# Local attention fused with a PReLU feed-forward network: half of each visit's block transfers go over GpSimd's queue

## The chip, the core and the metric

The program runs on one core of a Trainium2 chip. The core has four compute engines (PE, the matrix engine; DVE, the vector engine; ACT, the scalar engine; POOL, GpSimd) and SP (SyncE), which here only issues DMA transfers. Each engine works through its own instruction list in order; a transfer is issued by one of the engines, and then runs on the core's 16 DMA engines. The metric is the device time of one execution in microseconds.

## The reference

```
scores = (q_chunk @ k_chunk.T) / 8            # batch 8, 8 heads, seq 576, chunks of 64, head size 64
attn   = exp(scores - max); attn /= sum + 1e-9
x      = attn @ v_chunk                       # as a matrix: 4608 tokens x 512
h      = x @ w_in                             # 512 x 2048
g      = max(h, 0) + alpha * min(h, 0)
out    = g @ w_out                            # 2048 x 512
```

All data are float32. Attention is local: a chunk of 64 tokens looks only at itself.

## The kernel before

**Blocks.** The 4608 tokens are nine blocks of 512, and each block is four sub-blocks of 128 tokens (two chunks) for the attention. Sub-blocks 0 to 7 are done at the start in an order written out by hand (the list START). The other 28 are done in 28 *visits* that are woven into the feed-forward work.

**Stages.** Blocks 0 to 2 go through the plain feed-forward form, up to about 306 us: `first_layer` (L421) forms 128 hidden units for 512 tokens in a PSUM tile `ps_h`; ACT takes its negative part (L406), DVE completes the PReLU (L409), ACT rounds it to a high part gh (L435), DVE forms the low part gl (L438); `ffn_out` (L457) multiplies both with w_out into the result tiles ps_oa and ps_ob. At the end of a block (and of a part of one) `store` copies these four results out (L491 on ACT, for two of them sometimes L489 on DVE), and only then may PE write the next block's results there. Blocks 3 to 8 go in three pairs with a form of seven products in place of eight (`first_product` L719, `second_product` L847). Its weights are sums of quarters of w_in and w_out. They are made in the plain stage by `combine` (16 times: DVE L615, L622 to L625, ACT L631 and DVE L632, in the scratch tiles ta and tb and the buffers raw and more) and written to DRAM by POOL (`keep_a`, L593, four stores for each tile pair). The pair stages stream them back through a ring of four buffers (`stream`, L656, on POOL's queue); a load is issued when PE is done with the ring buffer that it goes into.

**A visit.** PE forms the values of the sub-block two visits earlier (`attn_values`, L388), which needs that sub-block's transposed probabilities `pT`, and then the scores of a new one (`attn_scores`, L272), in the one PSUM tile `ps_a`. DVE takes the row maximum (L284), ACT scales it (L285) and does eight exponentials (L287); ACT copies the values out of the same PSUM tile (L402 in the plain stage's first visits, with DVE's L403 for the low part; L399 later), and this copy (or L403) frees the tile for the next visit. DVE normalises (L289 to L291) and transposes 32x32 squares into a tile `t` (L331). `attn_blocks` then issues eight transfers (L338) of 32 partitions x 256 numbers (32 KB) each: chunk c, source half i, destination half j. They put the squares onto the right partitions in `pT`. Both t and pT have two buffers. 14 visits lie in the plain stage (136 to 286 us), 8 in the first pair stage (306 to 388 us), 6 in the second (464 to 538 us).

**Order.** PE's order is written in the code and pinned from the plain stage's step 20 on. The orders of DVE, ACT, POOL and SP are chosen when the kernel is built, by a scheduler that takes the instruction which is ready first in its own estimate of the times. So an edit to a transfer can move instructions of other engines. `combine` is tied behind the softmax of the latest visit; nothing else in the loop ties its rows to their place.

Of the kernel before, what the change touches and what calls it, by code (L numbers as in the profile page):

```python
# [59 lines left out]
def tile_local_attention_prelu_ffn(  # L60
# [12 lines left out]
    nc = tc.nc  # L73
# [253 lines left out]
    def attn_blocks(s):  # L327

        pr = probs.pop(s)
        tb = stage.tile([P, 2, H, HALF], F32, name="t3", bufs=2)  # L330
        nc.vector.transpose(tb.rearrange("p j h t -> p h j t"), pr)  # L331
        pT = load.tile([P, 2, H, HALF], F32, name="pT", bufs=2)
        for c in range(2):
            for i in range(2):
                for j in range(2):
                    src = slice(c * C + i * HALF, c * C + (i + 1) * HALF)
                    dst = slice(c * C + j * HALF, c * C + (j + 1) * HALF)
                    nc.sync.dma_start(  # L338
                        out=pT[dst, i].rearrange("p h t -> p (h t)"),
                        in_=tb[src, j].rearrange("p h t -> p (h t)"),  # L340
                    )
        pdiag[s] = pT
# [185 lines left out]
    def visit_results(old, xo, new, sc3):  # L528
        if old is not None:
            attn_x(old, xo)  # L530
        if new is not None:
            attn_blocks(new)
# [526 lines left out]
```

## Time and profile before

| | before |
|---|---|
| times of three runs, us | 774.68, 775.44, 777.26 (median 775.44) |
| the profiled execution, us | 775.11 |
| its span in the trace, us | 773.3 |
| outside the span, us | 1.8 |
| PE busy, us (share) | 761.3 (98%) |
| DVE busy, us | 648.2 (84%) |
| ACT busy, us | 448.9 (58%) |
| POOL busy, us | 184.9 (24%) |
| granted TensorE clock | 1.00 |

The span is the time from the first to the last instruction in the trace; the 1.8 us outside are the difference to the execution's own time. Busy time of an engine counts its compute instructions and, on POOL, the issue of its transfers; SP's issues are not counted. A wait is idle time of an engine just before an instruction, with what ended it.

### The profile page before, as it was taken

How to read it: one execution, taken by the hardware profiler on the slowest of the kernel's cores; microseconds unless marked ns; L12 is line 12 of the kernel's file. 1: busy time of each engine (PE TensorE's matmuls, PEld its weight loads, DVE VectorE, ACT ScalarE, POOL GpSimd, SP SyncE). 2: the span in 40 equal slices, each digit the busy share in tenths (PEclk: the TensorE clock that was granted, in tenths of full speed). 3: DMA queues.
4: the chain of work that ended last, by engine and by line, in shares of the span. 5: the costliest groups of instructions: out<-in, count | busy, mean ns of one | idle time of the engine just before them, and what ended most of it. 6: DMA issues, size and time to landing. Idle time of an engine off the chain costs nothing.

```text
span 773.3 us, 15417 instructions
## 1 busy us (share of the span) xinstructions
PE 761.3 (98%) x5558; PEld 640.4 (83%) x5558; DVE 648.2 (84%) x1140; ACT 448.9 (58%) x1221; POOL 184.9 (24%) x304
## 2 busy tenths in 40 slices
PE   7999999999999999999999999999999999999998
PEld 6788888887878888888888888888888888888886
DVE  6999989997989976877899898777898977679784
ACT  6975555566666665665756446655564544354642
POOL 1153322342425230111112111111122122112110
PEclk9999999999999999999999999999999999999999
DMA  9869595566969685878775678876656765565574
GB/s 355 328 198 386 180 322 206 182 228 192 267 209 272 219 287 168 304 272 279 264 239 204 232 243 286 267 235 212 207 201 218 253 236 191 200 208 192 197 253 148
DMA packets 69323, 184.53 MB, mean 239 GB/s; under 512 B 10992, under 2 KB 18176, under 8 KB 69120
## 3 DMA queue, kind: packets, MB, share of 16 engines
q0 software_dynamic: 34336, 119.56, 45.1%
q1 hardware_dynamic: 34480, 63.20, 24.0%
q8 instruction: 44, 0.72, 0.4%
q10 hardware_dynamic: 432, 0.79, 0.3%
q14 instruction: 31, 0.25, 0.1%
HBM read 135.27 MB, written 42.99 MB: 231 GB/s over the span
## 4 chain that ended last, share of the span: by engine, by line
PE 75%; DVE 6%; DMA 6%; ACT 5%; SPq 5%; issue 2%; POOL 0%; DVEq 0%; ACTq 0%
PE ps_o L719 19%; PE ps_o L847 19%; PE ps_h L719 10%; PE ps_h L847 10%; PE ps_h L421 6%; SPq L338 4%; PE ps_oa L457 4%; PE ps_ob L457 3%; DMA pT<-t 2%; PE ps_a L388 2%; DMA raw<-w_in 1%; ACT wi L313 1%; PE ps_a L272 1%; DMA raw<-w_out 1%; ACT wo L313 1%
## 5 line engine op out<-in xcount | busy, mean ns | idle before, releaser
L421 PE MATMUL ps_h<-xh,wi 128*128 128x512 f32 x384 | 101.6, 384 | 0.2 <-ACT xh L373 0.2
L421 PEld LDWEIGHTS ps_h<-xh,wi 128*128 128x128 f32 x384 | 70.8, 187 | 13.0 <-ACT xh L373 0.4
L719 PE MATMUL ps_o<-wi,raw 128*128 128x512 f32 x336 | 79.1, 382 | 0.0
L719 PEld LDWEIGHTS ps_o<-wi,raw 128*128 128x128 f32 x336 | 62.5, 187 | 11.2
L675 ACT CAST gh<-wo 128x512 fp32r<-128x512 f32 x66 | 41.0, 620 | 47.4 <-PE ps_o L847 31.8
L287 ACT ACTIVATE pr<-ps_a,mx 128x64 f32<-128x64 f32 x224 | 67.1, 326 | 0.9
L457 PE MATMUL ps_oa<-wo,gh 128*128 128x512 f32 x192 | 58.5, 385 | 0.3 <-ACT more L491 0.2
L457 PE MATMUL ps_ob<-wo,gh 128*128 128x512 f32 x192 | 57.8, 381 | 0.3 <-ACT g L491 0.3
L435 ACT CAST gh<-g 128x512 fp32r<-128x512 f32 x48 | 30.2, 630 | 35.3 <-DVE g L409 31.4
L421 PE MATMUL ps_h<-xl,wi 128*128 128x512 f32 x192 | 50.5, 381 | 0.0
L676 DVE TENSOR_TENSOR gl<-wo,gh 128x512 fp32r<-128x512 f32 x63 | 43.2, 685 | 7.6 <-ACT gh L675 7.1
L287 ACT ACTIVATION_READ_ACCUMULATOR pr<-ps_a,mx 128x1 f32 x224 | 48.9, 218 | 0.0
L656 POOL DMA_DIRECT2D raw<-wi_a x42 | 22.3, 531 | 98.0 <-PE ps_o L719 54.2
L656 POOL DMA_DIRECT2D raw<-wo_a x42 | 22.2, 529 | 90.8 <-PE ps_o L847 51.0
L406 ACT ACTIVATE wo<-gh 128x512 f32<-128x512 f32 x24 | 15.2, 632 | 48.4 <-DVE gh L749 48.4
L457 PEld LDWEIGHTS ps_ob<-wo,gh 128*128 128x128 f32 x192 | 35.8, 187 | 7.0 <-ACT g L491 0.7
L675 ACT CAST ta<-wo 128x512 fp32r<-128x512 f32 x42 | 26.1, 621 | 26.6 <-PE ps_o L847 15.4
L421 PEld LDWEIGHTS ps_h<-xl,wi 128*128 128x128 f32 x192 | 35.8, 187 | 6.6 <-DVE xl L375 0.2
L457 PEld LDWEIGHTS ps_oa<-wo,gh 128*128 128x128 f32 x192 | 35.4, 187 | 7.1 <-ACT more L491 0.6
L719 PE MATMUL ps_o<-wi,wi 128*128 128x512 f32 x168 | 40.4, 383 | 0.0
L719 PE MATMUL ps_o<-wi,wo 128*128 128x512 f32 x168 | 40.4, 383 | 0.0
L719 PE MATMUL ps_h<-wi,raw 128*128 128x512 f32 x168 | 40.4, 382 | 0.0
(298 smaller groups left out, 2037.7 us busy)
## 6 DMA issues: line engine op xcount, KB each, us to landing
raw<-wi_a POOLq DMA_DIRECT2D x42, 512.0 KB, 4.6
raw<-wo_a POOLq DMA_DIRECT2D x42, 512.0 KB, 3.5
wi<-wi_a POOLq DMA_DIRECT2D x21, 512.0 KB, 3.9
wo<-wi_a POOLq DMA_DIRECT2D x21, 512.0 KB, 4.0
wi<-wo_a POOLq DMA_DIRECT2D x21, 512.0 KB, 3.5
wo<-wo_a POOLq DMA_DIRECT2D x21, 512.0 KB, 3.8
k_sb<-kT SPq DMA_DIRECT2D x28, 256.0 KB, 4.4
q_sb<-qT SPq DMA_DIRECT2D x28, 256.0 KB, 3.8
```

Of the source, the lines that this page charges most:

```text
L287: last = nc.scalar.activation(pr[:, g], sc3[:, g // NP, g % NP], AF.Exp, bias=mx[:, g], scale=SCALE, accum_out=sm[:, g])
L313: last = nc.scalar.activation(pr[:, g], sc3[:, g % 2, g // 2], AF.Exp, bias=mx[:, g], scale=SCALE, accum_out=sm[:, g])
L338: nc.sync.dma_start(out=pT[dst, i].rearrange("p h t -> p (h t)"), in_=tb[src, j].rearrange("p h t -> p (h t)"),)
L388: pe(nc.tensor.matmul(att[0][par * C:(par + 1) * C, c, hp * C:(hp + 1) * C], lhsT=v_sb[rows, h * C:(h + 1) * C], rhs=p[rows, :, par * NP + ...
L421: pe(nc.tensor.matmul(woven(hps), lhsT=wi[f][:, l, k * P:(k + 1) * P], rhs=woven(xx[:, k]), start=(i == 0 and k == 0), stop=(i == 2 and k ...
L435: nc.scalar.copy(gh, g)
L457: pe(nc.tensor.matmul(woven(o), lhsT=a[:, ts], rhs=woven(wo[f][:, l]), start=(f == first and i == 0), stop=(f == last and i == 2),))
L656: streamed[0] = nc.gpsimd.dma_start(out=f32(t), in_=units[side][n])
L675: hi = nc.scalar.copy(t_hi, t)
L676: return hi, nc.vector.tensor_tensor(t_lo, t, f32(t_hi), op=ALU.subtract)
L719: pe(nc.tensor.matmul(woven(ps), lhsT=w[:, l, k * P:(k + 1) * P], rhs=woven(xx[:, xl]), start=first and at == 0, stop=at == n - 1, skip_gr ...
L847: pe(nc.tensor.matmul(woven(ps[m]), lhsT=w[:, l, m * P:(m + 1) * P], rhs=woven(xx), start=i in (1, 5, 2) and j == 0 and n == 0, stop=j == ...
```

## The change

In `attn_blocks`, a transfer whose source half i is 1 is issued by GpSimd, and one whose source half is 0 by SyncE as before. Four of a visit's eight transfers move, 112 of 224 in all. Their sizes, sources and destinations stay.

```diff
@@ -335,7 +335,7 @@
                 for j in range(2):
                     src = slice(c * C + i * HALF, c * C + (i + 1) * HALF)
                     dst = slice(c * C + j * HALF, c * C + (j + 1) * HALF)
-                    nc.sync.dma_start(
+                    (nc.gpsimd if i else nc.sync).dma_start(
                         out=pT[dst, i].rearrange("p h t -> p (h t)"),
                         in_=tb[src, j].rearrange("p h t -> p (h t)"),
                     )
```

The order of PE's 2392 rows is the same. The other engines' lists move as the scheduler chose.

On POOL the moved transfers stand in line with the stores of `keep_a`. This is the piece around the visits whose transposed tiles are t_1968 and t_2138 (about 160 to 175 us); wi_a_133 and so on are units of the combined weights in DRAM.

```order
 L593 DMA wi_a_133<-more 128x2x256 x2
 L593 DMA wi_a_135<-more 128x2x256 x2
+L338 DMA pT<-t_1968 32x256 x4
 L593 DMA wi_a_136<-raw 128x2x256
 L593 DMA wi_a_137<-raw 128x2x256
 L593 DMA wi_a_140<-raw 128x2x256 x2
+L338 DMA pT<-t_2138 32x256 x4
 L593 DMA wi_a_139<-raw 128x2x256
 L593 DMA wi_a_138<-raw 128x2x256
```

Two sets of four transfers now stand ahead of stores that followed each other before.

On ACT, a piece around the end of block 0's second part (about 170 to 177 us). ps_oa and ps_ob are the two result tiles; L631 are casts of `combine`.

```order
 L406 ACTIVATE g<-ps_h 128x512
 L631 CAST raw<-tb 128x512
-L631 CAST more<-ta 128x512
-L435 CAST gh<-g 128x512
-L406 ACTIVATE g<-ps_h 128x512
-L491 COPY more<-ps_oa 128x512 x2
 L435 CAST gh<-g 128x512
 L491 COPY ob<-ps_ob 128x512
 L491 COPY g<-ps_ob 128x512
+L631 CAST more<-ta 128x512
+L491 COPY more<-ps_oa 128x512 x2
 L285 ACTIVATE mx<-mx 128x8
```

The two copies that empty ps_oa stood ahead of an L435 and of the copies that empty ps_ob; they are now behind these and behind the cast of ta, which is the last product of a `combine`.

On DVE, about 265 to 272 us, the rows from the transposition of one visit to the row maximum (L284) of the next. wo_1104 and wo_1477 are the two weight tiles of one `combine`. Before:

```order
L438 TENSOR_TENSOR gl<-g,gh 128x512
L615 TENSOR_TENSOR ta<-wo_1104 128x512
L615 TENSOR_TENSOR tb<-wo_1477 128x512
L409 SCALAR_TENSOR_TENSOR g<-g,rise,ps_h 128x512
L622 TENSOR_TENSOR tb<-ta,tb 128x256
L623 TENSOR_TENSOR ta<-ta 128x256
L624 TENSOR_TENSOR ta<-tb,ta 128x256
L438 TENSOR_TENSOR gl<-g,gh 128x512
L625 TENSOR_TENSOR tb<-tb,ta 128x256
L632 TENSOR_TENSOR raw<-ta,raw 128x512
L632 TENSOR_TENSOR more<-tb,more 128x512
L284 TENSOR_REDUCE mx<-ps_a 128x8
```

In the changed kernel, the rows that end with the same L284:

```order
L409 SCALAR_TENSOR_TENSOR g<-g,rise,ps_h 128x512
L622 TENSOR_TENSOR tb<-ta,tb 128x256
L438 TENSOR_TENSOR gl<-g,gh 128x512
L623 TENSOR_TENSOR ta<-ta 128x256
L624 TENSOR_TENSOR ta<-tb,ta 128x256
L438 TENSOR_TENSOR gl<-g,gh 128x512
L625 TENSOR_TENSOR tb<-tb,ta 128x256
L632 TENSOR_TENSOR raw<-ta,raw 128x512
L615 TENSOR_TENSOR ta<-wo_1104 128x512
L632 TENSOR_TENSOR more<-tb,more 128x512
L284 TENSOR_REDUCE mx<-ps_a 128x8
```

The second L615 of this `combine`, and its L622 to L625, now stand behind L284; the rows L622 to L625 here belong to the `combine` before it, which before was done already while ACT worked on the exponentials of the visit before.

## Rows read from the trace of the kernel before

**Rows 1.** Windows: us, then busy us and (instructions) of each engine, clock, DMA, GB/s.
```profile
160.00:280.00 120.00, 117.55 (x1191) 97.28 (x1184) 107.53 (x210) 74.98 (x272) 46.73 (x63) 1.00 0.76 234
280.00:760.00 480.00, 480.00 (x3053) 405.25 (x3052) 389.51 (x638) 266.00 (x654) 89.62 (x169) 1.00 0.68 233
...
sum 773.30, PE 761.28 PEld 640.43 DVE 648.17 ACT 448.92 POOL 184.87; mean PE 152.26 PEld 128.09 DVE 129.63 ACT 89.78 POOL 36.97
```

**Rows 2.** Waits of PE: total us, times, longest; those from the first visits on.
```profile
PE ps_a L388 <- ACT xl L399: 0.9, 2, 0.5
...
PE ps_a L388 <- PE ps_h L421: 0.7, 1, 0.7
...
PE ps_a L388 <- DMA pT<-t: 0.4, 1, 0.4
PE ps_ob L457 <- ACT g L491: 0.3, 1, 0.3
...
PE ps_oa L457 <- ACT more L491: 0.2, 1, 0.2
```

**Rows 3.** Instructions of L338, the transfers of the change (SPq is SyncE's queue).
```profile
L338 SPq DMA_DIRECT2D pT<-t x224: 507/589/1837, 147.1 to 529.6; - x112
...
DMA to landing us min/median/max: 1.7/3.7/5.6
```

**Rows 4.** Groups of POOL: line, shape and count, busy us, mean ns, idle before.
```profile
L656 POOL DMA_DIRECT2D raw<-wi_a x42 | 22.3, 531 | 98.0 <-PE ps_o L719 54.2 <-PE ps_h L719 29.2 <-issue 6.2
...
L593 POOL DMA_DIRECT2D wi_a<-wi x24 | 18.1, 754 | 35.7 <-DVE wi L209 35.5
...
L638 POOL DMA_DIRECT2D partial<-more x4 | 4.7, 1184 | 0.0
```

**Rows 5.** Timeline of ACT near 170 us: start, duration, instruction, [idle before].
```profile
166.09 0.20 ACT L285 ACTIVATE mx<-mx 128x8 f32<-128x8 f32 x1
...
168.66 0.62 ACT L402 CAST xh<-ps_a 128x512 fp32r<-128x512 f32 x1
...
171.21 0.62 ACT L631 CAST raw<-tb 128x512 fp32r<-128x512 f32 x1 [1.42 <-DMA wi_a<-raw]
...
173.27 1.06 ACT L491 COPY more<-ps_oa 128x512 f32<-128x512 f32 x2
```

**Rows 6.** Timeline of DVE, same stretch.
```profile
164.52 0.68 DVE L284 TENSOR_REDUCE mx<-ps_a 128x8 f32<-128x512 f32 x1
...
180.31 0.69 DVE L291 TENSOR_TENSOR pr<-pr,sm 128x512 f32<-128x512 f32 x1
180.92 0.68 DVE L403 TENSOR_TENSOR xl<-ps_a,xh 128x512 fp32r<-128x512 f32 x1
```

**Rows 7.** Timeline of PE, same stretch.
```profile
174.98 0.60 PE L457 MATMUL ps_oa<-wo,gh 128*128 128x512 f32 x2
...
176.78 0.71 PE L457 MATMUL ps_ob<-wo,gh 128*128 128x512 f32 x2 [0.32 <-ACT g L491]
...
181.71 0.87 PE L388 MATMUL ps_a<-pT,v_sb 64*64 64x64 f32 x29 [0.68 <-PE ps_h L421]
```

**Rows 8.** Timeline near 272 us, DVE.
```profile
268.26 0.42 DVE L623 TENSOR_TENSOR ta<-ta 128x256 f32<-128x256 f32 x1
...
271.38 0.68 DVE L284 TENSOR_REDUCE mx<-ps_a 128x8 f32<-128x512 f32 x1
```

**Rows 9.** The same stretch, PE.
```profile
275.35 0.84 PE L388 MATMUL ps_a<-pT,v_sb 64*64 64x64 f32 x29 [0.55 <-ACT xl L399]
```

**Rows 10.** Timeline of DVE at the end of the plain stage.
```profile
301.59 0.68 DVE L438 TENSOR_TENSOR gl<-g,gh 128x512 fp32r<-128x512 f32 x1
```

**Rows 11.** Timeline of PE at that end.
```profile
303.61 0.38 PE L457 MATMUL ps_oa<-wo,gl 128*128 128x512 f32 x1
```

**Rows 12.** Timeline of POOL, one load in the pair stage.
```profile
315.48 0.53 POOL L656 DMA_DIRECT2D wi<-wi_a  x1 [2.11 <-PE ps_h L719]
```

**Rows 13.** Timeline of PE, first use of that load.
```profile
324.24 1.48 PE L719 MATMUL ps_o<-wi,wi 128*128 128x512 f32 x6
```

## Prediction

> **What bounds the kernel now.** I read the windows first, then PE's waits, then the timelines of the three engines around those waits. The windows are to show that PE is the bound: it is busy for 761.3 of 773.3 us, all of 280 to 760 us without a gap, and 117.55 of 120.00 between 160 and 280 us, at a granted clock of 1.00 throughout [rows 1]. The transfers of L338 are issued from 147.1 to 529.6 us [rows 3]; of PE's idle time only the 2.45 us from 160 to 280 us lie there, and the other 9.5 us come before the first visit or after 760 us, which the change doesn't reach. PE's waits [rows 2] give the 2.45 us names: 0.9 in two waits for the copy L399 that frees ps_a, 0.7 for L403, which frees the same tile (the table names PE itself there, but DVE's L403 begins at 180.92, lasts 0.68, and PE's L388 starts at 181.71 [rows 6, 7]), 0.4 for the transfers themselves, and 0.3 and 0.2 for the copies L491 that empty the result tiles. Their idle sums to 2.5 us. **That is the ceiling of a gain: 2.5 of 775, or 0.32%.** Only 0.4 of it is a wait for a transfer of the kind that is changed.
>
> Since PE's own order is the same, the time after is the time before, plus what PE waits more, minus what it waits less. PE has so little slack to win that the question is what new wait appears.
>
> **The transfers alone.** SP needs 0.589 us for an issue (median), so eight take 4.7 us, four 2.4; a transfer lands 3.7 us after its issue [rows 3]. SyncE's half of a pT is therefore complete some 2.4 us sooner. The trace has no L338 on POOL. The nearest row is a load of 128 rows, 0.531; a store of L593 costs 0.754, an accumulating one 1.184 [rows 4]. With 32 rows a moved transfer should cost no more than the load; I take 0.53, so four cost 2.1 us, and keep 0.75 to 1.18 (3.0 to 4.7 us) as the upper bound. A cost below nothing is excluded, since POOL does issue them. If POOL is free, both halves are complete 2.4 us sooner; if two stores stand ahead (1.5 us), 0.9 us sooner. So PE's wait of 0.4 us on a transfer goes away. I also expect the 0.2 us ahead of it to go, since the string of copies there is not longer than before: **-0.6 us**.
>
> **The pair stages.** Behind the four issues on POOL stands a load of the ring. POOL waits 2.11 us for PE before such a load, issues it at 315.48, and PE first uses it at 324.24, 8.76 us later [rows 12, 13]. The issues of a visit begin when its transposition ends and take 2.1 us, of which at most about 1.1 us fall on the moment of the next load. A load that took 6 us to land would still have 1.6 us over: **0**. At 1.18 an issue four take 4.7 us, and two or three loads would lose up to 3.6 us; then the slack of the tightest ones is gone, which goes into the slow rival.
>
> **Place A, the store at 165 to 182 us.** The rows that the scheduler moved matter more than the transfers. Before, ACT does two casts of a combine, then the softmax, and copies ps_oa out at 173.27 to 174.33 [rows 5]; PE's next write into ps_oa, at 174.98, finds that done [rows 7]. After, ACT goes straight to the softmax: DVE's L284 ends at 165.20 [rows 6], so L285 runs at about 165.24 and not at 166.09, 0.85 sooner, and the eight exponentials end at about 167.8 instead of 168.66. DVE then normalises (about 1.1 us to L403, by the 0.61 from L291 to L403 [rows 6] and two short rows) and begins L403 at 168.9. From there to the end of L623 its new list has nine rows: L403, L409, L331, L632, L438, L615, L622, L409, L623. Seven of 512 columns at 0.61 to 0.66 make 4.4 us, two of 256 at 0.42 to 0.46 [rows 8] make 0.9; with gaps of 0.2, L623 ends at 174.4. ACT's cast raw<-tb waits for it, and behind that cast, as the order shows, stand L435, the two copies out of ps_ob, the cast more<-ta, and only then the two copies out of ps_oa. Two such copies take 1.06 us, 0.53 each [rows 5]: 174.4 + 5 x 0.53 + 1.06 = 178.1. PE's write into ps_oa moves from 174.98 to 178.15, **a new wait of 3.17 us**. What it swallows: the wait of 0.32 at 176.78, since ps_ob is emptied sooner, and that of 0.68 at 181.71, since PE now comes later to L388 than L403 ends (about 183.1 by the same walk); from start to start of PE's rows these two cost 1.3 us. Net 3.17 - 1.3 = **+1.9 us**. Bounds: 0 if ACT's string ends 3.2 us sooner than I walk it, +3.0 if the store ahead of raw<-tb comes late too (that cast waited 1.42 us for a store already [rows 5], and on POOL four moved transfers now stand ahead of stores).
>
> **Place C, 252 to 277 us.** DVE's list from one visit to the next now does a combine half a visit later. Before, L615 to L624 of a combine filled DVE's wait for the exponentials; after, only L624 and L625 do, and the rest stands ahead of L284. By the same prices L284 of the visit at 271.38 [rows 8] comes 0.7 us later; ACT's exponentials come as much later, and an L406 of 0.5 us now stands among them. L399 ends at about 276.55 instead of 275.3, and PE's L388, which starts at 275.35 after a wait of 0.55 [rows 9], starts at 276.6. The first of L399's two waits (about 0.3) is already in this. **+1.25 us**, bounds 0 and +2.
>
> **The end of the plain stage.** DVE works off what was pushed back. Its last L438 starts at 301.59 and ends at 302.27; PE reads that gl at 303.61 [rows 10, 11], 1.3 us later. By my walk DVE is here about 3 us behind its old times, PE 1.25 us (relative to the shift of place A, which moves both). 302.27 + 3.0 = 305.25 against 303.61 + 1.25 = 304.86: **+0.4 us**, bounds 0 and 1.5.
>
> **Sum**: 1.9 - 0.6 + 1.25 + 0.4 = 2.95. The profiled execution took 775.11 us, 0.3 below the median of 775.44: 775.1 + 2.9 = **778.0 us**, 0.33% above the median. A measurement of this kernel tells changes above about 0.3% (2.3 us) from none.
>
> **A rule that speaks against the change.** The stores that POOL issues while DVE works on the weights cost 0.754 each, those loads that it issues beside a half idle DVE 0.531, for transfers of other shapes [rows 4]. The Trainium skill, page "SBUF — State Buffer", in the box on the "DVE blocks DMA" trap of its section "SBUF: two separate sides", says that a transfer issued by GpSimd has its descriptors written by GpSimd's own cores, and that these are locked out while DVE runs certain operations on two ports, so that such a transfer can stall where one from SP or ACT would not. By that rule the moved halves would land late; no row here shows an issue or a landing held up by DVE, and my sum goes without.
>
> **Rivals.**
> 1. *No measurable change.* The walk is exact to a microsecond or so, and its two large terms come from an order of which only the rows, not the times, are known. If place C brings nothing (an L284 on time), or if DVE gets through its nine rows 1.5 us sooner, the sum is +0.5 to +2.2: about 776.5 us. For it: 1.25 us at C rest on 0.7 us of an L284. Against: the copies out of ps_oa stand last in a string of six, which no small shift undoes.
> 2. *Faster.* The pT complete 2.4 us sooner, the softmax 0.85 us sooner, all waits of rows 2 vanish and none comes: 775.1 - 2.5 = 772.6 us. It decides at 174.98: ACT's string of casts and copies would have to end 3.2 us before my 178.15.
> 3. *Clearly slower, POOL late.* An issue of L338 costs 0.75 to 1.18 on POOL. Then the stores behind four of them come 0.9 to 2.6 us later, the buffers raw come free later, and the cast raw<-tb at place A, which waited for such a store before, takes the whole string with it: 778.9 to 780.6 us.
> 4. *Late landing.* Descriptors that wait for DVE would make a moved transfer land some 2 us later, near the slowest of today, 5.6 in place of 3.7 [rows 3]. Then the wait on pT at 222 us doesn't vanish but grows, by about 0.9 us: 778.9 us. This is what the rule of the page named above would do.
>
> That the change doesn't do what it says is excluded: the order shows four of a visit's rows on POOL.
>
> **How the numbers follow.** My forecast 0.40, rival 1 0.36, rival 2 0.06, rival 3 0.12, rival 4 0.06. The forecast's own range is 777.2 to 778.9, of which about a sixth lies within 2.3 us of the median. Faster: 0.06. Same: 0.36 + 0.06 = 0.42. Slower: 0.52. The range from 774.6 to 780.8 leaves out the faster rival and the end of the slow ones.
>
> **What would show it.** Right: in the profile after, a PE wait of about 3 us at an L457 into ps_oa near 178 us, released by ACT's L491; no wait on pT near 222 us; a wait of over 1 us for L399 near 276 us; 280 to 760 us nearly without a gap; L338 on POOL with a mean near 0.5 us. Wrong: PE's busy time in 160 to 280 us still above 117 of 120 (rival 1 or 2), an L338 above 0.75 us on POOL with waits for stores at L631 (rival 3), a wait on pT (rival 4), or a wait for a load in the pair stages.

## The result, and the profile after

The changed kernel takes 781.31 us (median of 6 runs, 779.94 to 783.80); the kernel before took 775.32 in the same comparison. The ratio is **1.0071**, 95% interval 1.0057 to 1.0086: slower by 0.71%, which is 5.5 us (the two medians lie 6.0 us apart). 778.0 was forecast, with 780.8 as the upper end: the direction and the places were right, the size was about half, and the time lies above the range. The profiled execution took 781.17 us, its span is 779.4 us against 773.3. The ratios in this document leave out one slow execution, of 2010.97 us, in one of the experiments (the changed kernel without two hold-ups).

Windows of the changed kernel first; columns as in [rows 1].

```profile
160.00:280.00 120.00, 113.84 (x1104) 93.79 (x1093) 100.20 (x196) 71.98 (x267) 63.86 (x99) 0.99 0.73 220
280.00:310.00 30.00, 30.00 (x187) 25.57 (x188) 26.68 (x46) 17.15 (x43) 11.53 (x19) 0.94 0.67 237
310.00:760.00 450.00, 450.00 (x2916) 379.75 (x2915) 364.94 (x597) 248.75 (x613) 113.94 (x218) 1.00 0.69 234
```

PE now stands still for 6.2 us between 160 and 280 us, 2.45 before [rows 1]. From 310 to 760 us it is busy without a gap, as before. New is the column of the clock: 0.99 and 0.94 where it was 1.00. The waits, to be read beside [rows 2]:

```profile
PE ps_oa L457 <- ACT more L491: 3.4, 2, 2.8
PE ps_a L388 <- ACT xl L399: 2.7, 2, 2.0
```

The waits for L403 and for pT are gone, and those for L491 and L399 have grown to 3.4 and 2.7 us. The transfers themselves, beside [rows 3]:

```profile
L338 SPq DMA_DIRECT2D pT<-t x112: 507/582/2012, 147.0 to 533.3; - x112
L338 POOL DMA_DIRECT2D pT<-t x112: 496/505/929, 147.4 to 533.6; - x112
...
DMA to landing us min/median/max: 1.7/3.5/8.1
```

An issue costs 0.505 us on POOL (median; the group's mean is 0.534), the price that was taken. Landing takes 3.5 us instead of 3.7. No wait of PE names pT. A moved transfer landed 3.7 us after its issue (median), one of SyncE's 3.2; between 160 and 280 us the two are 3.0 and 2.8.

**Place A.** Timeline of ACT, beside [rows 5]:

```profile
165.14 0.21 ACT L285 ACTIVATE mx<-mx 128x8 f32<-128x8 f32 x1
...
174.16 0.62 ACT L631 CAST raw<-tb 128x512 fp32r<-128x512 f32 x1 [2.68 <-DVE tb L623]
...
176.16 0.63 ACT L631 CAST more<-ta 128x512 fp32r<-128x512 f32 x1
176.68 1.08 ACT L491 COPY more<-ps_oa 128x512 f32<-128x512 f32 x2
```

and of PE, beside [rows 7]:

```profile
177.81 0.99 PE L457 MATMUL ps_oa<-wo,gh 128*128 128x512 f32 x2 [2.84 <-ACT more L491]
178.60 0.63 PE L457 MATMUL ps_oa<-wo,gl 128*128 128x512 f32 x1
...
181.56 0.60 PE L457 MATMUL ps_ob<-wo,gh 128*128 128x512 f32 x2
...
184.96 0.69 PE L388 MATMUL ps_a<-pT,v_sb 64*64 64x64 f32 x32
```

This is the string of the forecast, within 0.35 us: the softmax begins at 165.14 (165.24 was walked), raw<-tb at 174.16 (174.4), the copies out of ps_oa end at 177.76 (178.1), and PE's write starts at 177.81 (178.15). But from 177.81 on the rows are long: two matmuls take 0.99 us where two took 0.60 [rows 7]. Windows around the two long waits:

```profile
176.00:178.00 2.00, 0.19 (x1) 0.19 (x2) 1.43 (x3) 1.76 (x4) 2.00 (x4) 1.00 0.95 344
178.00:180.00 2.00, 2.00 (x6) 1.54 (x6) 0.11 (x1) 1.82 (x12) 1.85 (x3) 0.53 1.11 413
...
182.00:184.00 2.00, 2.00 (x11) 1.69 (x10) 1.90 (x4) 0.62 (x1) 0.00 (x0) 1.00 0.51 202
276.00:280.00 4.00, 2.03 (x10) 1.38 (x9) 3.65 (x10) 3.74 (x20) 1.46 (x3) 1.00 0.75 283
...
282.00:284.00 2.00, 2.00 (x5) 1.61 (x6) 2.00 (x4) 0.00 (x0) 2.00 (x4) 0.52 0.42 145
284.00:286.00 2.00, 2.00 (x10) 1.67 (x10) 2.00 (x5) 0.17 (x1) 2.00 (x5) 1.00 0.83 255
```

TensorE's clock fell from its upper level (2.4 GHz) to its lower (1.2 GHz) about when PE came out of each wait, and was up again by the last windows shown. From the end of the wait to L388 PE took 7.15 us (177.81 to 184.96); the same rows at the upper level take 5.50 in a run shown below. **No term of the sum held this.** In the five profiles in which the clock fell here, PE took 6.99 to 8.45 us for these rows; in the four with the moved rows of A in which it stayed up, 5.48 to 5.52. At place B (first fence) and place C (second), PE:

```profile
222.50 0.72 PE L457 MATMUL ps_oa<-wo,gh 128*128 128x512 f32 x2 [0.55 <-ACT more L491]
...
225.36 0.69 PE L388 MATMUL ps_a<-pT,v_sb 64*64 64x64 f32 x32
```

```profile
256.46 0.84 PE L388 MATMUL ps_a<-pT,v_sb 64*64 64x64 f32 x29 [0.70 <-ACT xl L399]
...
279.95 0.99 PE L388 MATMUL ps_a<-pT,v_sb 64*64 64x64 f32 x29 [1.97 <-ACT xl L399]
...
284.26 0.62 PE L457 MATMUL ps_ob<-wo,gh 128*128 128x512 f32 x2
```

### The profile page after: what moved, and what is told of

Same layout as the page of the kernel before. It is cut to its first block, busy times and chain, and to the rows that moved or that the text cites. A ratio compares the mean times of both kernels' runs of the same rounds, so it can differ in the third digit from the quotient of the medians.

```text
span 779.4 us, 15558 instructions
## 1 busy us (share of the span) xinstructions
PE 763.0 (98%) x5558; PEld 641.4 (82%) x5558; DVE 648.5 (83%) x1140; ACT 448.8 (58%) x1221; POOL 241.5 (31%) x416
## 4 chain that ended last, share of the span: by engine, by line
PE 73%; DVE 9%; ACT 8%; DMA 7%; issue 2%; POOL 1%; ACTq 0%; DVEq 0%; SPq 0%; POOLq 0%
PE ps_o L719 19%; PE ps_o L847 19%; PE ps_h L719 10%; PE ps_h L847 9%; PE ps_h L421 5%; PE ps_oa L457 4%; PE ps_ob L457 3%; ACT pr L287 3%; DMA wi_a<-raw 2%; DMA wo<-qT 2%; PE ps_a L388 1%; DMA raw<-w_in 1%; DVE gl L438 1%; DVE g L409 1%; DMA wo_a<-more 1%
## 5 line engine op out<-in xcount | busy, mean ns | idle before, releaser
L421 PE MATMUL ps_h<-xh,wi 128*128 128x512 f32 x384 | 101.7, 385 | 0.3 <-ACT xh L373 0.2
L421 PEld LDWEIGHTS ps_h<-xh,wi 128*128 128x128 f32 x384 | 70.8, 187 | 13.3 <-DVE g L409 0.5
L719 PE MATMUL ps_o<-wi,raw 128*128 128x512 f32 x336 | 79.1, 382 | 0.0
L719 PEld LDWEIGHTS ps_o<-wi,raw 128*128 128x128 f32 x336 | 62.5, 187 | 11.2
L338 POOL DMA_DIRECT2D pT<-t x112 | 56.8, 534 | 28.7 <-DVE t L331 8.5
L457 PE MATMUL ps_oa<-wo,gh 128*128 128x512 f32 x192 | 60.2, 394 | 3.5 <-ACT more L491 3.4
L457 PE MATMUL ps_ob<-wo,gh 128*128 128x512 f32 x192 | 58.1, 383 | 0.0
L421 PE MATMUL ps_h<-xl,wi 128*128 128x512 f32 x192 | 50.5, 381 | 0.0
L435 ACT CAST gh<-g 128x512 fp32r<-128x512 f32 x48 | 30.2, 629 | 34.4 <-DVE g L409 33.5
L457 PEld LDWEIGHTS ps_oa<-wo,gh 128*128 128x128 f32 x192 | 36.0, 191 | 11.1 <-ACT more L491 4.2
L406 ACT ACTIVATE wo<-gh 128x512 f32<-128x512 f32 x24 | 15.2, 632 | 48.4 <-DVE gh L749 48.4
L457 PEld LDWEIGHTS ps_ob<-wo,gh 128*128 128x128 f32 x192 | 36.3, 189 | 6.7
L421 PEld LDWEIGHTS ps_h<-xl,wi 128*128 128x128 f32 x192 | 35.8, 187 | 6.6 <-DVE xl L375 0.2
L719 PE MATMUL ps_o<-wi,wi 128*128 128x512 f32 x168 | 40.4, 383 | 0.0
L719 PE MATMUL ps_o<-wi,wo 128*128 128x512 f32 x168 | 40.4, 383 | 0.0
```

The source lines that it names most:

```text
L338: (nc.gpsimd if i else nc.sync).dma_start(out=pT[dst, i].rearrange("p h t -> p (h t)"), in_=tb[src, j].rearrange("p h t -> p (h t)"),)
L406: nc.scalar.activation(g, h, AF.Relu, scale=-1.0)
L421: pe(nc.tensor.matmul(woven(hps), lhsT=wi[f][:, l, k * P:(k + 1) * P], rhs=woven(xx[:, k]), start=(i == 0 and k == 0), stop=(i == 2 and k ...
L435: nc.scalar.copy(gh, g)
L457: pe(nc.tensor.matmul(woven(o), lhsT=a[:, ts], rhs=woven(wo[f][:, l]), start=(f == first and i == 0), stop=(f == last and i == 2),))
L719: pe(nc.tensor.matmul(woven(ps), lhsT=w[:, l, k * P:(k + 1) * P], rhs=woven(xx[:, xl]), start=first and at == 0, stop=at == n - 1, skip_gr ...
```

## The experiments

DVE's and ACT's orders differ between the two kernels at three places: near 165 to 177 us (34 lines of difference on DVE, 25 on ACT; **A**), near 200 us (13 and 8; **B**), and from 240 us on (141 and 82; **C**). Built with single visits moved, the orders show that each place hangs on one visit: A comes when the second visit's four transfers go over GpSimd, B with the fifth, C with the ninth. So queue and order can in part be taken apart by the condition in one line:

```diff
-                    (nc.gpsimd if i else nc.sync).dma_start(
+                    (nc.gpsimd if i and s - EARLY not in (1, 8) else nc.sync).dma_start(
```

s - EARLY counts the visits from 0. In each run below "moved" means four of a visit's eight transfers on GpSimd. Two theories stood against each other: the moved rows (and the clock behind their waits), and the transfers themselves. All ratios are to the kernel before on the same chip. No run has the moved rows with all transfers on SyncE: that the rows cost the time, and not the four transfers that move them, is read from the waits.

The profiles allow a finer comparison. From PE's first L719 to its last L847 every profile takes 462.11 or 462.12 us, and ACT's first L285 of the visits begins somewhere between 140.35 and 142.86 us, at 141.21 and 141.92 in two profiles of the same kernel. What is left is **the stretch** from that L285 to that L719: 165.70 us before, 171.98 in the changed kernel.

**26 visits moved**, all but the second and ninth (the diff above).

> 26 of the 28 visits send half of their transfers over GpSimd's queue; the second and the ninth visit send all eight over SyncE's. DVE's and ACT's instruction orders are then row for row those of the kernel before. Theory (the time comes from the rows that the scheduler moved on DVE and ACT, and from the TensorE clock that the long waits cost): no wait of 2.8 us at 175 us, none of 2 us at 278 us, granted clock 1.00, time 774.5 to 775.6, like before or up to 0.7 us less since the wait on a transfer at 222 us is gone. Rival (the transfers themselves, by their issue on GpSimd and their landing): 26/28 of the +6.0 us, 780.9.

Measured: 1.0014 (1.0000 to 1.0027), clock 1.00, waits as expected but for one of 1.0 us into ps_oa near 220 us. The expectation was wrong on one point: the orders were not quite those of before, since B was in. So most of the cost went away with A and C, and 1.1 us stayed.

**Two visits moved**, the second and sixth: `s - EARLY in (1, 5)`.

> Only the second and the sixth visit send half of their transfers over GpSimd, 8 of 224 transfers in all. DVE's and ACT's orders then differ from before at one place only, the store near 175 us, as in the changed kernel. Theory: the wait of 2.84 us for the copies out of ps_oa and the slow clock behind it return in full, 2.84 + 1.2 - 1.0 = +3.0 us: 778.3, granted clock at half for some 3 us after the wait. Rival (the transfers): 2/28 of +6.0 us, 775.7.

Measured: 1.0033 (1.0020 to 1.0047), a wait of 2.9 us into ps_oa and clock 0.91 from 160 to 200 us. 8 transfers of 224 cost 2.5 us, where the theory of the transfers had 0.4.

**26 visits moved, C in, A and B out**: `s - EARLY not in (1, 4)`.

> 26 visits send half of their transfers over GpSimd, all but the second and the fifth. DVE's and ACT's orders are then those of before up to about 240 us and those of the changed kernel after that. Theory: the waits for L399 near 253 and 276 us grow by 1.9 us together, and the clock costs 1.4 us after the second: +3.3 less 0.4 to 0.7 for the wait at 222 us, 777.9 to 778.6. Rival (the transfers): as in the run that keeps both orders, whatever that gives.

Measured: 1.0032 (1.0022 to 1.0042), 2.5 us, waits for L399 of 2.7 us together; in the profiled execution the clock stayed at 1.00 behind them. Within the theory's range for the waits, below it for the clock: this profile's mean clock is 0.997, but the half clock lies near 18 us, before the first visit.

**Both waits filled with work**: the changed kernel with 12 matmuls ahead of the first-layer products at A, and 8 behind those at C.

```diff
+    extra = lambda hps, f, xh, m: [pe(nc.tensor.matmul(woven(hps), lhsT=wi[f][:, 0, :P],
+        rhs=woven(xh[:, k % NK]), start=k == 0, stop=k == m - 1)) for k in range(m)]
...
+        passes = [(0, xh), (0, xl), (1, xh)]; extra(hps, f, xh, again)
...
+        next(parts); extra(ps_h.tile([P, TB], F32, name="ps_h") if unused else None, f, x[0], unused)
...
+        pending.append((acc, ffn_in(x[b], f, {27: 12}.get(n, 0), {43: 8}.get(n, 0)), f, f0, f1, b, False))
```

> The changed kernel with 20 more matmuls of 128x512 whose results are not used: 12 ahead of the first-layer products before the wait near 175 us, 8 ahead of the wait near 278 us, 4.4 us of work in the 4.8 us that PE waits there. Theory (the clock falls to its lower level because PE idles there, and stays low for some 3.5 us each time): more work and less time, 781.3 - 1.2 - 1.4 = 778.7, granted clock 1.00. Rival (PE is slow there for another reason, such as the transfers that run at the same time): no gain, 781.3 or up to 2 us more where the extra products don't fit into the wait.

Measured: 1.0049 (1.0033 to 1.0064), clock 1.00 in four of five executions, 0.998 in one. 4.4 us more work, and no more time than the changed kernel. That the time fell is not shown: the intervals overlap. (The profile with 0.998 has its half clock near 16 us, ahead of the visits.) At C the added matmuls waited 1.4 us themselves (for L409, which frees their PSUM tile), so that wait was not filled as meant.

Then each place alone, and none.

**25 visits moved**, A, B and C out: `s - EARLY not in (1, 4, 8)`. DVE's and ACT's orders are those of before, row for row.

> 25 of 28 visits send half of their transfers over GpSimd, all but the second, the fifth and the ninth. DVE's and ACT's orders are now row for row those of before (the run with 26 visits still had a difference of 13 lines near 200 us). Theory (only the moved rows cost time): 0 to -0.7 us against before, no clock loss. Rival (the four issues on GpSimd, 2.0 us a visit, hold up the stores behind them, and so the buffers raw and the casts of combine): the +1.1 us of the run with 26 visits stays, and a wait of about 1 us for the copies out of ps_oa near 220 us with it.

Measured: 1.0017 (1.0007 to 1.0027), +1.3 us: the rival. POOL and ACT of this run:

```profile
175.85 2.00 POOL L338 DMA_DIRECT2D pT<-t  x4
...
179.33 0.99 POOL L499 DMA_DIRECT2D partial<-g  x1
...
204.71 2.41 POOL L338 DMA_DIRECT2D pT<-t  x4
206.72 1.88 POOL L593 DMA_DIRECT2D wi_a<-raw  x2
```

```profile
184.95 0.60 ACT L406 ACTIVATE g<-ps_h 128x512 f32<-128x512 f32 x1 [0.83 <-DMA partial<-g]
...
208.02 0.62 ACT L631 CAST raw<-tb 128x512 fp32r<-128x512 f32 x1 [1.26 <-DMA wi_a<-raw]
```

The four issues of the third visit take 2.0 us ahead of L499, and L406, which writes the buffer that L499 reads, waits 0.83 us for it. Those of the sixth take 2.4 us ahead of two stores, and L631 waits 1.26 us for their buffer. PE's waits, to be compared with those of the run with 23 visits:

```profile
PE ps_a L388 <- ACT xl L399: 1.6, 2, 1.1
...
PE ps_oa L457 <- ACT more L491: 1.1, 1, 1.1
```

**Only the second visit moved** (A alone): `s - EARLY in (1,)`.

> Only the second visit sends half of its transfers over GpSimd, 4 of 224. DVE and ACT differ from before at the store near 175 us alone (34 and 25 lines of difference), as in the changed kernel. Theory: as much as the run with two visits, +2.5 us, with a wait of 2.8 us or more into ps_oa and half clock for some microseconds behind it. Rival (the transfers): 1/28 of +6, 0.2 us.

Measured: 1.0042 (1.0027 to 1.0058), +3.3 us from four transfers.

```profile
PE ps_oa L457 <- ACT more L491: 2.9, 1, 2.9
...
PE ps_a L388 <- ACT xl L399: 0.8, 2, 0.6
```

**Only the fifth** (B alone): `s - EARLY in (4,)`.

> Only the fifth visit sends half of its transfers over GpSimd. DVE and ACT differ from before near 200 us alone (13 and 8 lines). If that piece of the order is what cost the run with 26 visits its 1.1 us, +1.1 us here, with a wait of about 1 us into ps_oa near 220 us; if the stores held up on GpSimd cost it, about 0.

Measured: 1.0012 (1.0000 to 1.0024), 0.9 us, with a wait of 1.0 us into ps_oa near 220 us. ACT of this run:

```profile
202.59 0.62 ACT L631 CAST raw<-tb 128x512 fp32r<-128x512 f32 x1 [2.78 <-DMA wi_a<-raw]
...
218.72 1.08 ACT L491 COPY more<-ps_oa 128x512 f32<-128x512 f32 x2
```

In the new order DVE's L632 of the second raw buffer comes behind L615 and L438, ACT's cast waits 2.78 us for a store, and the copies out of ps_oa start at 218.72 instead of 217.97 before.

**Only the ninth** (C alone): `s - EARLY in (8,)`.

> Only the ninth visit sends half of its transfers over GpSimd. DVE and ACT differ from before from about 240 us on (141 and 82 lines), as in the changed kernel. Theory: the waits for L399 near 253 and 276 us grow by 1.9 us, +1.9 us, and up to 1.4 us more in executions in which the clock falls after the second. Rival (the transfers): 0.2 us.

Measured: 1.0038 (1.0024 to 1.0051), +2.9 us. The one wait for L399 is 2.0 us, as in the changed kernel:

```profile
PE ps_a L388 <- ACT xl L399: 2.0, 1, 2.0
```

The execution with clock 0.999 took 777.24 us; the other five, at 0.997, 778.01 to 779.71. Where the clock fell in those five no trace tells.

**A alone, its wait filled** (12 matmuls as above, the second visit moved).

> The kernel in which only the second visit sends half of its transfers over GpSimd, with 12 more matmuls of 128x512 (unused results, 2.6 us) ahead of the first-layer products before the wait near 175 us. Theory (the wait into ps_oa costs 2.9 us less what later waits give back, and the half clock behind it 1.2 to 2.4 us more): the extra work lies in the wait and the clock stays at its upper level, so PE comes to the next visit 1.2 to 2.4 us sooner; of that, part goes into waits that PE then meets sooner, 0.5 to 2.0 us less than the run without the extra work, ratio to before 1.0016 to 1.0036. Rival (no clock effect): ratio 1.0042 or more.

Measured: 1.0032 (1.0020 to 1.0044), clock 1.00 in seven of nine executions. It lies in the theory's range, and its interval touches that of the run without the extra work (1.0027 to 1.0058): inconclusive on the time. The profiles speak for the rival: the stretch is 167.56 us without the extra work, where PE took 7.14 us from the wait to L388, and 167.61 with it, where PE took 5.50. By the end of the plain stage nothing can be told any more of the half clock behind this wait.

**The changed kernel, the wait at A filled.**

> The changed kernel with the same 12 matmuls at the same place, and none at the second wait. Theory: 0.5 to 2.0 us less than the changed kernel, ratio to before 1.0045 to 1.0065; half clock only behind the second wait, near 278 us. Rival (no clock effect): 1.0071 or more.

Measured: 1.0074 (1.0061 to 1.0086): no gain. PE of this run:

```profile
173.17 2.91 PE L164 MATMUL ps_h<-xh,wi 128*128 128x512 f32 x12
...
178.95 0.73 PE L457 MATMUL ps_oa<-wo,gh 128*128 128x512 f32 x2 [0.22 <-ACT more L491]
...
215.48 0.84 PE L388 MATMUL ps_a<-pT,v_sb 64*64 64x64 f32 x29 [0.62 <-ACT xh L399]
...
223.47 0.73 PE L457 MATMUL ps_oa<-wo,gh 128*128 128x512 f32 x2 [1.13 <-ACT more L491]
```

The 12 matmuls (L164) lie in the wait, of which 0.22 us is left, and the rows behind it are short. But PE then meets waits at 215.48 and 223.47, of 0.62 and 1.13 us, where the changed kernel has none at the first and 0.55 at the second. Nor did the extra work hold them up: ACT's string was as late at 165.66, ahead of the added matmuls, as at its end (1.1 us behind the changed kernel's profile in both). ACT ends the copies out of ps_oa near B some 44 us after the L285 that follows the copies at A, whether the clock fell at A (44.30, 43.98 and 44.61 in the changed kernel, its repetition and the run with its orders alone) or not (44.13 here, 44.19 with both waits filled, 43.99 without the hold-ups). So PE waits there for ACT, and what the clock takes at A is hidden.

**Only the pair stages moved**, the last 14 visits: `s >= EARLY + 14`.

> Half of the transfers go over GpSimd in the 14 visits of the pair stages alone; DVE's and ACT's orders are those of before. Theory (the cost lies in the plain stage, in moved rows and in stores held up on GpSimd; in the pair stages the loads behind the transfers have microseconds to spare): no wait of PE from 310 to 760 us, ratio 1.000. Rival (the transfers themselves cost, everywhere): half of what 25 visits cost, 1.0008, with waits for a load L656.

Measured: 1.0002 (0.9993 to 1.0010).

```profile
160.00:280.00 120.00, 117.60 (x1225) 97.41 (x1222) 107.23 (x210) 75.12 (x272) 46.47 (x62) 1.00 0.76 230
...
310.00:760.00 450.00, 450.00 (x2858) 379.88 (x2858) 369.44 (x604) 248.84 (x611) 115.20 (x220) 1.00 0.72 234
```

Not a gap from 310 to 760 us: the forecast of 0 for the pair stages holds.

**23 visits moved**, B, A, C and the two hold-ups out: `s - EARLY not in (1, 2, 4, 5, 8)`.

> As the run with 25 visits, but the third and the sixth visit too send all over SyncE: on GpSimd the four issues of the third stood ahead of the accumulating transfer L499 (which ACT's L406 then waited 0.8 us for), those of the sixth ahead of two stores of a buffer raw (which L631 waited 1.3 us for). Orders on DVE and ACT as before. Theory (these two hold-ups are the +1.3 us of that run): back to before or up to 0.7 us less, ratio 0.999 to 1.0005, and the wait into ps_oa near 220 us back to about 0.2 us. Rival (the price of the transfers spread over all visits): 23/25 of it, 1.0016.

Measured: 1.0004 (0.9995 to 1.0013).

```profile
PE ps_a L388 <- ACT xl L399: 1.6, 2, 1.1
...
PE ps_oa L457 <- ACT more L491: 0.2, 1, 0.2
```

The wait into ps_oa is back at 0.2 us from 1.1, and the time at that of before. The intervals of the two runs overlap a little, but the profiles agree with the ratios: the stretch is 167.21 us with the two hold-ups and 165.98 without. So the +1.3 us were those two hold-ups. The wait for pT near 222 us is gone, and PE pays for that with 1.6 us for L399 where it had 0.9 [rows 2]: it only comes sooner to the next engine that is late.

**The orders of the changed kernel, 12 transfers moved**: `s - EARLY in (1, 4, 8)`.

> Only the second, the fifth and the ninth visit send half of their transfers over GpSimd, 12 of 224. DVE's and ACT's orders are then row for row those of the changed kernel, and no transfer on GpSimd stands ahead of the stores that were held up. If the moved rows explain all of the +0.71%, ratio 1.0071; if the held-up stores of the third and sixth visit add their 1.3 us to them, about 1.0054; if they lie under the waits that the moved rows make, 1.0071 again.

Measured: 1.0075 (1.0053 to 1.0097).

```profile
PE ps_oa L457 <- ACT more L491: 3.9, 2, 2.9
PE ps_a L388 <- ACT xl L399: 2.0, 1, 2.0
```

**The changed kernel without the two hold-ups**: `s - EARLY not in (2, 5)`.

> The changed kernel, but the third and the sixth visit send all over SyncE: orders on DVE and ACT row for row those of the changed kernel, 104 of its 112 transfers on GpSimd. If the hold-ups of these two visits add to the moved rows, 1.0054, as the run with three visits; if the other 100 transfers cost something as well, more than that run.

Measured: 1.0064 (1.0047 to 1.0081). In the profiled execution the clock did not fall:

```profile
177.06 0.71 PE L457 MATMUL ps_oa<-wo,gh 128*128 128x512 f32 x2 [2.31 <-ACT more L491]
...
182.56 0.70 PE L388 MATMUL ps_a<-pT,v_sb 64*64 64x64 f32 x32
...
278.92 0.84 PE L388 MATMUL ps_a<-pT,v_sb 64*64 64x64 f32 x29 [1.97 <-ACT xl L399]
...
281.67 0.60 PE L457 MATMUL ps_ob<-wo,gh 128*128 128x512 f32 x2
```

```profile
174.00:177.00 3.00, 0.75 (x4) 0.31 (x2) 2.43 (x5) 3.00 (x7) 1.79 (x3) 1.00 0.43 121
177.00:179.00 2.00, 1.94 (x9) 1.67 (x10) 0.36 (x1) 1.58 (x11) 2.00 (x3) 1.00 0.90 268
...
274.00:279.00 5.00, 3.03 (x15) 2.26 (x14) 4.66 (x11) 3.77 (x20) 2.42 (x4) 1.00 0.86 336
279.00:281.00 2.00, 2.00 (x67) 1.82 (x68) 2.00 (x4) 1.93 (x4) 0.53 (x1) 1.00 0.00 0
```

The wait into ps_oa was 2.31 us here, and from its end to L388 PE took 5.50 us; the clock was at its upper level behind both waits. At C PE took 2.75 us from the end of the wait to the row into ps_ob (278.92 to 281.67), where the changed kernel takes 4.31 (279.95 to 284.26). Two executions with a mean clock of 0.999 and 1.000 took 779.35 and 780.32 us; three at 0.993 took 781.51 to 782.31, 2.0 us more on average. Only the first of the five was traced.

**The changed kernel beside them.**

> The changed kernel itself beside these two on the same chip: 1.0071, and in its profile the same waits (2.8 us into ps_oa near 178 us, 2.0 us for L399 near 280 us).

Measured: 1.0064 (1.0048 to 1.0079), waits of 2.9 and 1.9 us, half clock behind both. So 12 transfers out of 112 give all of the slowdown that can be told, through the rows that the scheduler moved. The hold-ups, worth 1.3 us where the orders are those of before, seem to lie under the waits that the moved rows make: 1.0064 with and without them, each known to 0.0017 (1.3 us), and, with the clock up, a stretch of 170.85 us with them (the run with A filled) and 170.68 without.

## Why the prediction was right in kind and wrong in size

PE's order is the same in both kernels, so one PE row can be timed in each. The table gives the start of five rows, and, in brackets, how much later that is than before. The last column is the profile of the run without the two hold-ups, which has the changed kernel's orders on DVE and ACT, and in which the clock stayed up. In that profile ACT's string at A also began 0.76 us sooner (L285 at 164.38), before any half clock, so the two last columns do not differ by the clock alone.

| PE row | before | changed kernel | without hold-ups, clock up |
|---|---|---|---|
| L457 | 40.02 | 39.74 (-0.3) | 39.63 (-0.4) |
| L457, behind place A | 183.03 | 186.05 (+3.0) | 183.65 (+0.6) |
| L421, behind place B | 223.80 | 226.45 (+2.65) | 225.40 (+1.6) |
| L457, behind place C | 276.64 | 281.83 (+5.2) | 280.22 (+3.6) |
| last L847 | 769.10 | 775.30 (+6.2) | 773.23 (+4.1) |

From these differences, by the terms of the forecast:

| term | forecast | changed kernel | without hold-ups, clock up |
|---|---|---|---|
| place A | +1.9 | 3.0 + 0.3 = +3.3 | 0.6 + 0.4 = +1.0 |
| 183 to 224 us | -0.6 | -0.4 | +1.0 |
| place C | +1.25 | +2.5 | +2.0 |
| the rest of the plain stage | +0.4 | +1.0 | +0.5 |
| sum | +2.95 | +6.5 | +4.5 |

- **PE as the bound, the ceiling of a gain, the pair stages at 0**: right. No run was faster than before, and the pair stages alone gave 1.0002.
- **The issue price** of 0.53 us: right, 0.534 (mean).
- **Place A**: the mechanism was right, and the new wait was mis-sized by little (3.17 walked, 2.84 found; 2.31 in the third column).
- **183 to 224 us**: the step that failed first. The -0.6 us was wrong. That pT comes sooner is right (no wait for it any more), but "the string of copies there is not longer than before" was not walked: the fifth visit's rows (B) move an L632 behind two others, and the casts and copies come late, +0.9 us alone. ACT ends the copies near B 81.23 us after its first L285, where it was 77.76 before. Up to B the sum had +1.3 us (1.9 - 0.6); the table gives +2.9 with the half clock and +2.0 without. That the changed kernel has -0.4 on this line, near the forecast, is luck: the half clock at A had made PE late already.
- **The clock**: the missing term, and the second step that failed. The sum took a wait to cost what PE stands still. In [rows 1] the clock was 1.00 everywhere, but PE's longest wait in that stage was 0.7 us [rows 2], so those rows said nothing of waits of 2 and 3 us. The half clock behind A took 7.15 - 5.50 = 1.65 us, but PE gives it back at B, where it waits for ACT at either clock. The half clock behind C took 4.31 - 2.75 = 1.56 us, and behind it nothing gives much back. Net it is worth about 1 us: the stretch is 171.98 and 171.64 us in the two profiles of the changed kernel, 170.85 and 170.68 in those of its orders with the clock up (171.39 where it fell at A alone, in a run that also waits 0.6 us for pT; 171.56 with both waits filled, where the added work at C itself makes PE 1.5 us late). The added work did not settle this by the time, whose intervals overlap.
- **Place C**: right in kind, 2.0 us instead of 1.25. L399 ends 0.62 us after its start at 279.27, so at 279.9; the forecast's 276.55 lies 3.3 us sooner, of which 2.65 us are PE's own lag by then. Of the +2.5 in the table 0.6 us are already half clock.
- **The end of the plain stage**: +0.4 was to be a wait for the last gl. The changed kernel has no such wait (PE is busy for 30.00 of 30 us from 280 to 310); its +1.0 is the rest of the half clock behind C. With the clock up the wait is there, 0.3 us. The term looks half right by luck.
- **Rival 3** (stores held up on POOL) is real in another form: not by a dearer issue, but by 2.0 us for four at the price taken, ahead of L499 and of two stores. Alone it is 1.3 us, in the changed kernel little or nothing.
- **Rival 4**, the rule of the Trainium skill (page "SBUF — State Buffer", section "SBUF: two separate sides"), is not borne out: between 160 and 280 us, where DVE is busy for 100.20 of 120 us, transfers issued by POOL landed in 3.0 us (median) and those by SP in 2.8, and PE waited for none. No run shows whether DVE's rows here are of the kind that the page means. The loads with which the prediction compared the stores were not issued beside a half idle DVE either: it was busy for 389.51 of 480 us there [rows 1].

The Trainium skill's page "DMA: Bandwidth & Descriptors", in its section "Issuing engines are not separate DMA queues", says that issuing from several engines saves only the time of issue. Over the whole run the trace agrees: landing went from 3.7 to 3.5 us at the median. Between 160 and 280 us it went from 3.6 to 2.8, which is more, and no run here tells why.

## What to carry to other kernels

Where a scheduler orders the engines by its own estimates, an edit of one transfer is an edit of every engine's order: compare the orders first, find which part of the edit releases which moved piece, and time those. When most of an edit can be kept without the moved pieces (23 of 28 visits here, 1.0004), the transfers as such are not what costs; their place in a queue can be, as with the third and the sixth visit. And a new wait of some two microseconds or more on TensorE is to be priced with the clock that may fall behind it; then ask which engine would have made PE wait next, since that can hide all of it, as at A, or next to nothing, as at C.

## What the hardware showed that was not expected

Whether the clock falls behind a wait was not settled by the wait's length between 1.9 and 2.3 us. Behind the wait for L399 of 1.9 to 2.0 us it fell in both profiles of the changed kernel, and stayed up in five others: 26 visits with C, the ninth visit alone, the filled wait at A, the 12 transfers, and without the hold-ups. Behind the 2.31 us at A in the last of these it stayed up as well. Behind a wait into ps_oa of 2.84 to 2.90 us it fell in all five profiles that have one; in the run with two visits it fell some 0.8 us before PE came out, and there PE took 8.45 us to L388.

The mean clock of an execution doesn't say where it fell. In four profiles (26 visits with C, both waits filled, 23 visits, the 12 transfers) it was 0.59 to 0.69 from 16 to 20 us, ahead of all visits, and 1.00 there in the kernel before. The run with 23 visits has a mean of 0.997 from that alone, and its executions at 0.997 (775.40 to 776.55 us) are no longer than those at 1.000 (775.42 to 777.53). So that the same program takes two times some 2 us apart, as the executions without the hold-ups suggest, is likely but not shown. Why the clock falls in some executions and not in others stays open; no run here tells.
